# Another written order, with its PSUM slots and masks, for threshold attention followed by a three-way maxout FFN

## The chip, the cores and the metric

The kernel runs on one core of one Trainium2 chip. The metric is the device time of one execution in microseconds, as the median of several runs. The engines are PE (TensorE; its weight loads are shown as PEld), DVE (VectorE), ACT (ScalarE), POOL (GpSimd) and SP (SyncE), which issues nearly all DMAs.

## The reference

Attention over 8 batches of 8 heads, 576 rows of 64 each, in which each row of scores keeps only what lies within tau of its maximum; then an FFN whose hidden layer is the maximum of three products.

```python
scores = scale * np.matmul(q, k.transpose(0, 1, 3, 2))
thresh = np.max(scores, axis=-1, keepdims=True) - tau
scores = np.where(scores >= thresh, scores, -1000000000.0)
attn = np.exp(scores - np.max(scores, axis=-1, keepdims=True))
attn = attn / (np.sum(attn, axis=-1, keepdims=True) + 1e-09)
x = np.matmul(attn, v)                     # heads side by side: 4608 rows of 512
h = np.maximum(np.maximum(x @ w1, x @ w2), x @ w3)   # 768 wide
out = h @ w_out
```

## The kernel before

The work is cut into 16 quads (8 batches, two quads of four heads each). A quad has 9 chunks of 128 rows, each for two heads at once; a chunk has two halves r, one for each head of its pair, so there are 288 scores of 128 x 576 in all.

The functions, in the order in which a chunk meets them: `load` (SP) brings q, k and v of a quad; `transposed` (PE, tile `tp`) turns q and k, and `evacuated` (ACT for q, DVE for k) copies them to `qt` and `kt`; `swapped` (POOL, at the start DVE too) makes `qs`, q with the two halves of the partitions exchanged. `scores` (PE, tile `sc`) makes a score as two matmuls, one on each half of the array's rows, 256 columns on the one and 320 on the other, in two passes each. `maximum` (DVE) reads the score from PSUM, writes it negated to `z` and its row minimum to `nm`.

From there a score half goes one of two ways, and each way has two forms. Its digit in the string `MASKED` says which:

- 0, plain: `threshold` (DVE, a 128 x 1 instruction, `th`), `exponents` (ACT, reads `z`), `numerators` (ACT, a second pass with a sum).
- 1, masked: `exponents` (ACT, once), then `numerators` on DVE, which drops what is below exp(-tau) and sums.
- 2 and 3, direct: as 0 and 1, but ACT's `exponents` reads the score from PSUM and not from `z`; no threshold is made for 2. The bank then comes free only behind ACT.

`reciprocals` (DVE, `rs`), `normalized` (POOL, `P`) and `turned` (SP, a transposing DMA from `P` to `ptq`) follow. `product` (PE, tile `o`) multiplies with the values when all chunks of a quad have landed, and ACT or DVE copies the result to `xt`. The FFN of a batch (`ffn`) starts when both quads of it are in `xt`: 18 hidden products (`ph`, each in two steps of eight matmuls on alternating row halves), of which ACT copies one in three and DVE takes the maximum with the other two, then the output products (`po`), which ACT copies to `ob`.

All PSUM tiles share four slots of two banks each (`bank`, tags s0 to s3). What sets the order is neither a scheduler nor a planner in the kernel: the string `ORDER`, some 2,900 letters, is read from left to right, and each letter issues the next piece of its kind; `_Ordered` chains all instructions of an engine in that order. S, T, O, F and N stand for score, transposes, value product, FFN piece and ninth-chunk output, each with the digit of its slot; B is the second step of an FFN piece. m, s, e, n and k are maximum, threshold, exponents and the numerators on ACT and DVE; r, p and t reciprocals, normalized and turned; a and c copies of q and k; q the swap; h and v the copies and maxima of hidden products; x and w the copies of value products; u, j and f those of outputs; l and y loads and casts of q, k and v; g and z loads and casts of the weights, through a staging pool of two buffers; o, i and d stores. An engine works strictly in its own order, so a piece that has to wait holds all behind it on that engine.

```python
while x < len(text):
    what = text[x]
    if what in "STOFN":
        x += 1
    issue(what, int(text[x]) if what in "STOFN" else None)
    x += 1
```

Of the kernel before, what the change touches and what calls it, by code (L numbers as in the profile page):

```python
# [39 lines left out]
ORDER = """  # L40
llllllglllT0laclT1laclzllqqS0qqS1meS2mS3lmlT0enlkS1ylmlT2eamelrnpS3leqlmnyS1qcapS0emtnrcS3pmnT2qmepgrelS1qya
gS0pmelT2mqnS3tcpemqS2nlkT1eytaS0rmnT1kpermS3yS2enczrmS1qT0enmepnqtS3nprmaymgpeS0lptS2mppT0mtpS1enencnqsS3re
rmtpS0mS1penmS3lqnsS2mtperpekzllmT0tmpenkT1pgS3eearnS0petmnqrS2meqlnpS3lmnplsS2cetpremS1pS0nmplermtzeS3mnS2p
mtnpmS3rkpS1leektS0emnrpmemptS1eekS2pO3mktS0rennmpermT2pnS1wptemS3prkyO0tmeakS2pgS1enxlnrmS0lpesS2mezT3mS1np
mgntspcS2eqrseT3mtpeS0srmapS1mnT2ptS3mnqO0ceqmeO1prswnptnkS3pxS0meF1meS2zBresmT0qghF3klpF2nkBtaS1sveS0pemF3B
nyrrsmyBepT1svS0hpcT2nS3zmaS1erpgsF2mntpsBmnS3yvF1etssT0myeBprS2cnpS3mnS0ympelF2epF3lmBnzslssvS0htBrqmeS2vpn
S1gF0sepmF3teqBmF2erssvpBtnBkphF0eS1vtS3znmF2nrBmqteS1rpvBnS3pmlnF0pmgeS1qsBsrhmS3pevS2npS1mF0npsO3ermpesmO2
zewepgsskBxtT3nF1vS2nklBarS0mlphS3mtepF2sS1rmnyBmetF3pvT0eBpcnS2tzT1nvS0asmzS3temS2qeS1meF0trkpmS3lenpBmnlys
reklpF1umerpskS3upBeoketmS0uS2umpS3tesmS1qeT0myO2nqlrsnlprcO3etqsmepwS0xptS1mnF3psnmS2BlerskpS1thF0meF3pmeBF
2ktnBveBsrS1nvpS0hmyF3emF2npBrssT0eprtvBaF1kS3nqvBeF0myhyS2kyleF3mBelBvnpS2snsS0vptemS1pnF3rmpT2tnBmpeF0scS1  # L50
htBrnmpF3erT2rpvlBasS1pstvnS2pmeF0pS3emtBqnmT2S1hcqS3empF2eS0rsqmtS1epsmBeF3pmnF0stsvBeBknF2klhF1BvelS0nrvpB
emT3pS2arvS0ptnS3mpnO1smtesrkpeF2swnlrpmeT0S1qtescS3epBmnpmnT0trskS3paS1umS0ulqmeS3lmyS1nopS2smelS0rmeS3psmn
O1ypersmqO2etkpemO0lewqxlknpS3tS1keF2momS3lexF0ktT1enkBercpnsBpumN1ertkphkF3jS0rursS1empBnmF2ptS0vpS1smeF3yt
BsnsmBpnvS0pT1hmF2atT3srepS0cF1eprBsmeqF3vnByBynvplS2nsS0plmhS1mteS2mF0nF3mteS1rrspBnmS2pelvBlepF1smT0leqBvl
aS2rkhF3oqnsS0mtS1epmBeqsF2ssmtS0epvBeyF1mnF3vpBesrS0ktphBermS1npT2svO0nytmpncT3eS1wF2nrmS0aBrsmnqF3vnT1pS0c
eBptsF2mhpS1eS3pmteS0qmBeO1spmnkteF3rvnpT0BsskapS2xvS0erS1qmtnS3pmnF2mqlespmeS1rtkBepresmT3puS1cuS0ptmnS3pS2
meyS1lrekpF0tnsmempO3lekteskO2nrsmpeBkpxrnwS1uptS3muS2pnmF0yoeS1mF3lesymBtnS2srkpS1hmBeF0spveF2ertBmpT3nrsvS
1paBlmpnS0tS3qhmF1epsmS2leBymF3tevF0nBknlS1rsvpS2esmqnBF3srmhpS1epS0tmeF2pssBrempBtesvS0ynF1mT3lnpBvF0lhsrcS
2tnT1mBnF3valS2nrBsqmeF0pvS1epS2meBptsmS3eqF1hmT2peBcS3tnskT2O0arkplnmO2lerpvewptS3xkpS1nF2meF0sstreBsmpS3nv
pBnmS1tS2hmT3eF0rmpnF1cBpnBrevptT3S2apvS0qmtS3S1enmqF2esrsqmiepmleS0soykeS1plBnmemtS3ukS0uT1snrlO2cpekynO1me  # L60
ymeF3pwxskteS0keS1BrrnkopmF2pmS0BqeuurtsmF1phS3srnpS2meT0ptBmeS3ykpaN2esvempF0tS1jkpF3ermBeS2ptvnS1pmBnS0rls
hsmpS2elF3mqntS1mpF0nsrBskpeF2lsmBetBpveF1yhvS3lnkS2lesF0mytnBmBerqsS3veF2lpvnF1pBsmT0htBceF3rT2vnpBsaS0pvnF
1qmtS2nBsrnmT0pS3hrcpF2esS1mpteS0rmpS3emBpntF1svqnS0ssBmpeoT2vO3lamtneF1wS0nrlBpmeS3qsrS2hsmS0pnmF1eptS3smeB
pmF2ntS0veS3rsmnpS1BnpO0veytrempS2empS3xsmS1tekF0nsknlT2rmpBelmlpnscS3quS1umyS2eorT0kpeO3tmeyO1ewlepsmF3etka
rknS2qklT0nBmxespcS2eryF0mpF1uskpuBtnS2BhmqF3nsvS0peS2srmtpF1eBmpeF0srvnBptS2hyS3pmeF1lmeBlBevtF3nkT2S0arrvp
BnS2mphS1smpF0ntS3smnpBmeF1lsT2esvlF3nrBrcptBnvpS2eS0qmlhS1tsnprsmT3F2epmS0aptBemF3yevS1oS0nqmBnpsrS2mnF1ptv
S0epmBeS3mthS2skeF0F1snmlBeklO3ersvpnrmByepF0swT2eqtBvnqF3ssrcS1hpiBmpT0S2vaptS1snmS0pnT3mqF2tecT1BarmS3pnS1
vqeS0mF2pesrmnptmS3npT1seS0qctBeymqermpS1eS3mpuF0nmtuskS1eS2klnS3smBesrsepO1upmemO2txrkpukeO3wnkpS0xS2emF3et
rmS1pnBssspmF2hS0rtepS3mnBpmF1etS0veF3mnN2rnpBpjF0evtF2esBkBkhF1nsvS3eBmBevO3hrkS2pwnS1mnF3prmS2eptsF0mnBpsS
1sevyS2terBmpeF3svS1iyepBmoS0yhmtF2ekF3nBsmS1ersBvpnF0pmeF2BvteS1hBmF3rsS0vpeF1rknpBBmnO2vhptO0xrpnS3pwS2trm  # L70
npS0mnF3pmteF1pBeBvtS0rS2vpS3empF1ktkF0kBereskpemBkperumO2uptO3xpN1wtenkO2jrF3pxF1hpF2nvF3tvF1rhF2pvF3pvF1hF
2tvF3vF1hF2voF3vF1ohF2vF3vF1hF2vO3vO1wF2xuuF1oF0hiF3vF1vF0hF3vF1vF0hF3vF1vF0hF3vF1vF0hF3vF1vF0huF3vF1ovF3uoF
0uoN1fjdi
"""


# [753 lines left out]
```

## Time and profile before

| what | value |
|---|---|
| median of 3 runs | 446.21 us (446.2 to 446.45) |
| span of the profiled execution | 444.8 us |
| PE busy | 422.4 us (95%) |
| ACT busy | 403.0 us (91%) |
| DVE busy | 392.8 us (88%) |
| POOL busy | 311.9 us (70%) |
| DMA | 88.50 MB, mean 199 GB/s |

The profiled execution's own time is its span, 444.8 us from the first to the last instruction; the runs' median is 1.4 us longer. In the profile's lines each instruction group is written as engine, operation and out<-in by the names above; all of the kernel's own instructions carry the line L93, since `_Ordered` records them there, so one reads them by tile.

### The profile page before, as it was taken

Reading aid. Unit: us, or ns where it says so; the run is one execution under the profiler, and the core shown is the slowest. Engines: PE = TensorE matmul, PEld = TensorE weight load, DVE = VectorE, ACT = ScalarE, POOL = GpSimd, SP = SyncE. Lnnn points to the kernel's source line nnn. Section 1 sums busy time; section 2 is a strip of 40 time slices with the busy share of each in tenths; the row PEclk is TensorE's granted clock in tenths of the full one; section 3 lists DMA queues with packets and bytes.
Section 4 is the critical chain, followed back from the end, with each engine's and each line's share of the span. In section 5 each row is a group of like instructions: output and inputs, shape, how many; then the busy total and the mean of one; then the engine's idle time right before and its main releaser. Section 6 shows DMA issues by size and latency. Waiting matters only on the chain.

```text
span 444.8 us, 14254 instructions
## 1 busy us (share of the span) xinstructions
PE 422.4 (95%) x5188; PEld 320.2 (72%) x5190; DVE 392.8 (88%) x1228; ACT 403.0 (91%) x836; POOL 311.9 (70%) x420
## 2 busy tenths in 40 slices
...
GB/s 188 275 293 199 291 169 269 235 243 262 229 180 194 212 222 292 125 256 167 143 234 189 230 198 203 209 168 210 208 206 194 244 151 105 83 179 136 145 116 108
DMA packets 213959, 88.50 MB, mean 199 GB/s; under 512 B 189184, under 2 KB 202240, under 8 KB 213888
## 3 DMA queue, kind: packets, MB, share of 16 engines
...
q8 instruction: 41, 0.67, 0.6%
q10 hardware_dynamic: 528, 0.62, 0.5%
...
## 4 chain that ended last, share of the span: by engine, by line
PE 86%; ACT 5%; DVE 4%; issue 2%; DMA 1%; SPq 0%; DVEq 0%; ACTq 0%
PE ph L93 32%; PE sc L93 32%; PE po L93 10%; PE o L93 9%; ACT z L93 5%; PE tp L93 3%; DVE z L93 3%; DMA qm<-in_q_dram 1%; ACT qt L93 1%; SPq L93 0%; DVE xt L93 0%; DVE hm L93 0%; DVE stage L93 0%; DVE rs L93 0%; ACT ob L93 0%
## 5 line engine op out<-in xcount | busy, mean ns | idle before, releaser
L93 POOL TENSOR_SCALAR P<-z,rs 128x576 bf16<-128x576 f32 x250 | 200.6, 814 | 63.3 <-DVE rs L93 28.1
L93 DVE TENSOR_SCALAR_CACHE_REDUCE z<-sc 128x576 f32<-128x576 f32 x250 | 183.7, 750 | 14.8 <-PE sc L93 10.1
L93 PE MATMUL sc<-kt,qs 64*128 64x256 f32 (+2 forms) x640 | 182.6, 423 | 5.7 <-DVE z L93 2.3
L93 PE MATMUL sc<-kt,qt 64*128 64x320 f32 (+2 forms) x640 | 182.4, 433 | 5.2 <-ACT z L93 3.3
L93 PE MATMUL ph<-xt,w 64*128 64x288 bf16 (+2 forms) x2160 | 170.8, 283 | 0.1
L93 PEld LDWEIGHTS <-w 64*128 64x128 bf16 (+1 forms) x2160 | 130.1, 94 | 28.6 <-issue 4.3
L93 ACT ACTIVATE z<-z 128x576 f32<-128x576 f32 x174 | 117.6, 679 | 0.1
L93 PEld LDWEIGHTS sc<-kt,qs 64*128 64x128 f32 (+1 forms) x640 | 92.4, 180 | 25.7 <-DVE z L93 5.7
L93 ACT ACTIVATE z<-z,th 128x576 f32<-128x576 f32 x143 | 106.2, 769 | 5.0 <-DVE th L93 4.2
L93 PEld LDWEIGHTS sc<-kt,qt 64*128 64x128 f32 (+1 forms) x640 | 91.9, 179 | 19.7 <-ACT z L93 5.9
L93 DVE SCALAR_TENSOR_TENSOR z<-z 128x576 f32<-128x576 f32 x76 | 62.2, 830 | 0.5 <-ACT z L93 0.5
L93 PE MATMUL po<-wo,hT 64*128 64x512 bf16 (+3 forms) x454 | 53.5, 354 | 0.3
L93 POOL COPY qs<-qt 64x640 f32<-64x640 f32 (+3 forms) x66 | 43.0, 652 | 10.8 <-ACT qt L93 7.2
L93 ACT ACTIVATE z<-z,nm 128x576 f32<-128x576 f32 x68 | 50.6, 767 | 0.0
L93 DVE TENSOR_TENSOR hm<-ph,hm 128x576 bf16<-128x576 f32 (+2 forms) x54 | 37.0, 686 | 9.2 <-PE ph L93 8.9
L93 ACT ACTIVATE hm<-ph 128x576 bf16<-128x576 f32 (+2 forms) x54 | 31.8, 589 | 13.4 <-PE ph L93 12.8
L93 POOL TENSOR_SCALAR P<-stage,rs 128x576 bf16<-128x576 f32 x38 | 30.4, 804 | 19.3 <-ACT z L93 5.4
L93 PEld LDWEIGHTS <-hT 64*128 64x128 bf16 (+2 forms) x456 | 30.0, 95 | 16.5 <-issue 2.3
L93 DVE TENSOR_TENSOR hT<-ph,hm 128x576 bf16<-128x576 f32 (+2 forms) x54 | 37.0, 686 | 4.0 <-PE ph L93 2.3
L93 PE MATMUL o<-ptq,vb 128*64 128x64 bf16 (+2 forms) x544 | 39.0, 281 | 0.0
L93 ACT ACTIVATION_READ_ACCUMULATOR z<-z 128x1 f32 x174 | 34.3, 197 | 0.0
L93 PEld LDWEIGHTS <-vb 128*64 128x64 bf16 x544 | 23.3, 111 | 12.8 <-issue 4.9
...
## 6 DMA issues: line engine op xcount, KB each, us to landing
...
qm<-in_q_dram SPq DMA_DIRECT2D x15, 512.0 KB, 5.0
km<-in_k_dram SPq DMA_DIRECT2D x15, 512.0 KB, 5.3
out_dram<-ob SPq DMA_DIRECT2D x14, 512.0 KB, 4.0
stage<-in_moe_w_dram SPq DMA_DIRECT2D x9, 512.0 KB, 5.2
ptq<-P SPq DMA_TRANSPOSE x144, 4.0
...
stage<-in_moe_w_out_dram SPq DMA_DIRECT2D x3, 512.0 KB, 4.9
```

The costliest lines, as they stand in the source:

```text
L93: ins = fn(*a, **kw)
```

## The change

The two strings are replaced: `MASKED`, 288 digits, and `ORDER`, which has the same pieces in another order and with other slot digits. Nothing else differs; no matmul, load or store is added or taken away. The digits change in number too: 169 plain, 78 masked, 33 and 8 direct before; 184, 82, 14 and 8 now. So DVE makes 90 masked sums instead of 86, ACT 198 second passes instead of 202, and 184 thresholds stand in place of 169. Of the 41 direct reads of PSUM 37 stood ahead of the first hidden product; of 22, 13 do.

```diff
 MASKED = """
-232222322322222222021032222202332122123122200200111000000000100000000011
...
+000300021200000210020001210102023030023000211010000100000010000001001010
...
 ORDER = """
-llllllglllT0laclT1laclzllqqS0qqS1meS2mS3lmlT0enlkS1ylmlT2eamelrnpS3leqlmnyS1qcapS0emtnrcS3pmnT2qmepgrelS1qya
...
+llllllgllT2lcaqqlT2S3alcqqmgS1zsS3mesnmS1gS0emlS3snmlT2ermS0plaseslpmnlcqS1skeqlT3canmqS3zleS2mnqrmS3eplS0my
...
```

Where it moves instructions, at three places. The first is DVE's list from its third instruction of the program's start on, with the copies of the first transposes (`kt`, `qs`) and the first maxima (`z,nm<-sc`); before:

```order
L93 COPY kt<-tp 128x320
L93 COPY qs<-qt 64x320
L93 COPY qs<-qt 64x256
L93 TENSOR_SCALAR z,nm<-sc 128x576 x3
L93 TENSOR_SCALAR z,sm<-z 128x576
L93 TENSOR_SCALAR z,nm<-sc 128x576 x2
L93 RECIPROCAL rs<-sm 128x2
```

and now:

```order
L93 COPY kt<-tp 128x320
L93 COPY qs<-qt 64x320
L93 COPY qs<-qt 64x256
L93 TENSOR_SCALAR z,nm<-sc 128x576
L93 TENSOR_SCALAR th<-nm 128x1
L93 TENSOR_SCALAR z,nm<-sc 128x576
L93 TENSOR_SCALAR th<-nm 128x1
L93 TENSOR_SCALAR z,nm<-sc 128x576 x2
L93 TENSOR_SCALAR th<-nm 128x1
```

The first maxima are now followed by thresholds (`th`), which the direct form did not need; the first masked sum (`z,sm<-z`) comes later.

The second is SP's list, from the last load of the first quad's q on: `stage` are weights, `vm` and `vr` values, `q`, `qm` and `km` what `tp` needs next. Before:

```order
L93 DMA qm<-in_q_dram 64x2x512
L93 DMA vm<-in_v_dram 64x4x256
L93 DMA vm<-in_v_dram 64x4x256
L93 DMA vr<-in_v_dram 64x8x64
L93 DMA vr<-in_v_dram 64x8x64
L93 DMA q_147<-in_q_dram 128x2x64
L93 DMA k_149<-in_k_dram 128x2x64
L93 DMA qm<-in_q_dram 128x2x512
```

and now:

```order
L93 DMA qm<-in_q_dram 64x2x512
L93 DMA vm<-in_v_dram 64x4x256
L93 DMA stage<-in_moe_w_dram 128x4x256
L93 DMA stage<-in_moe_w_dram 128x4x256
L93 DMA vm<-in_v_dram 64x4x256
L93 DMA vr<-in_v_dram 64x8x64
L93 DMA vr<-in_v_dram 64x8x64
L93 DMA q_147<-in_q_dram 128x2x64
L93 DMA k_149<-in_k_dram 128x2x64
L93 DMA qm<-in_q_dram 128x2x512
```

Two weight loads have moved ahead of half of the values and of the second quad's q and k; the second of them waits for POOL, since the staging pool has two buffers.

The third is PE's list behind the first step of the first hidden product (`ph`). Before:

```order
L93 MATMUL ph<-xt,w_63 128x288
L93 MATMUL sc<-kt,qs 128x256
L93 MATMUL sc<-kt,qt 128x320
L93 LDWEIGHTS w_63
L93 MATMUL ph<-xt,w_63 128x288
```

and now:

```order
L93 MATMUL ph<-xt,w_63 128x288
L93 MATMUL tp<-identf,km 128x64 x8
L93 MATMUL sc<-kt,qt 128x256
L93 MATMUL sc<-kt,qs 128x320
L93 MATMUL sc<-kt,qt 128x320
L93 MATMUL sc<-kt,qs 128x256
L93 MATMUL tp<-identf,qm 128x64 x8
```

The transposes of keys (`tp<-identf,km`) of the fourth quad and two more scores, which stood ahead of this product, now stand behind its first step.

More of the change, by code (lines that the diff above doesn't have):

```diff
@@ L24 @@
 MASKED = """
-232222322322222222021032222202332122123122200200111000000000100000000011
-000010111020011000101000000001100001001000010011111100000000100100000000
-110010030111000100010000000001010100001110001011010100110000000000000000
-100101101011000000120000001010000000110011100000001110001000010011111021
+000300021200000210020001210102023030023000211010000100000010000001001010
+000011001100010101001000000000101000101020101111010110000000010000001001
+010011101010210100100001000100110000000001110101030110000001000000001000
+000111000111010023001000000010000000111201010011011100000011000100031312
 """
@@ L40 @@
 ORDER = """
-llllllglllT0laclT1laclzllqqS0qqS1meS2mS3lmlT0enlkS1ylmlT2eamelrnpS3leqlmnyS1qcapS0emtnrcS3pmnT2qmepgrelS1qya
[L42 to L70, printed above, removed]
@@ L71 @@
-npS0mnF3pmteF1pBeBvtS0rS2vpS3empF1ktkF0kBereskpemBkperumO2uptO3xpN1wtenkO2jrF3pxF1hpF2nvF3tvF1rhF2pvF3pvF1hF
-2tvF3vF1hF2voF3vF1ohF2vF3vF1hF2vO3vO1wF2xuuF1oF0hiF3vF1vF0hF3vF1vF0hF3vF1vF0hF3vF1vF0hF3vF1vF0huF3vF1ovF3uoF
-0uoN1fjdi
+llllllgllT2lcaqqlT2S3alcqqmgS1zsS3mesnmS1gS0emlS3snmlT2ermS0plaseslpmnlcqS1skeqlT3canmqS3zleS2mnqrmS3eplS0my
+nsmezersS1tpekS3lepT2mnlpasrmynS2ylqelT0npmlT1nspcT2arqrS3ectqeS2gmpnspS1nmT0eqmepsS1tapT3mnS2yesrS1mpeS0mtn
+pcS1ertsmpelmyepklnS1ynrsS3ptnmpeslrS2mpeT1mepS0tezmlnkqaS0ntmegrspS0npertS1mpnlknS0qsemS3qermT2tqeskS0gnpS1
@@ new lines @@
+mepcntmzO2elmnprnwS1pesmS2pterS3rmpleT0kpaS2mS1ntpssemS3lqeO0mlnkpemtxrsT3peS0cznS2rmntpeS0rpsmetpsmS2npkS3e
+tyemnS0rtmpeS2gmpnlmS0nyplskT1eS2yeO3rmtqarknpS0gsmeO1preswyemS2xtS3kpnlF0smeT1prmS2npcnS3zsmT1eBmapS2shsgF1
+qmeF3qBektBpnrS2vlnF0ympS1esBvpnS2trspmF3hlzmeBseT0svzT2tS1acgS3pnrF2mnpS0meT1qBmF3nytcpS0evBlperF1mgphS2ssk
+npS0tmeF3lBseqsmF2lnqrBveByvS1eS0ptmhS3lnpmF2nF1zsmBersS0pvnF3pmeBzBstnvS2hlrsS0pmeF3yrmpeF2tBknpS1veS0tmnBq
+gS3mnpS1lerrpsO0mepvteO3spwlnpsmleF2kyT0xS1kaBlnmS3hS0rsmpeS1tsrpS2melF3mqeT0mBynF1scnT2ptBvaS0pevS3zemS2tey
@@ new lines @@
+S1rmqnF0smtnpmeS3psBemqetkT1usS3knF2trcpusmepS1esS0ormpS3empBntmelkS1uS0lrmnpO3sukyntmO2qerwpetkS1pxlS0semS3
+lF2pnmF1lesrmBponS0rkplS3hmBleF2ymelF0sBvpeBkepF3rsntvS1BphmF2nyslpF0svnBrT3evlBaF1keS2qS3hmpBemF0qntS2rssve
+pS3mnBptrF1snvpS2emBptnS0mpF3hrmT2ptnBceF0vT1tBarsS2evlqS1nmF3pS0nsmtpBemS2qhT1ssmS0peS3cnytF2mnS1sBmetF0rve
+pF3mBeptS2srevplF1nsBmpF0ektBhkBleO2vlnrvpeT1rwpS3tnS0kpaF2snmpemtT1eS3rscpS0nmBqetmpeT1kS0arS3supmS1umtqnS0
+meqS3omS2npS1meS0rsmnpO3kemeO2ymxnpO1rwtepkeS0yS2remtpF3xsmpekS1qeS2smeBymepklnyF1T0kluBucN2hkteS0ornkpF3ljm
@@ new lines @@
+S1lBpsrsemS0lpevS2F1psmeT3tBmalF0vnT3BknS2chS1nrF0srpsmeF3prBsmeF2pnvtBqS1nsrvS0eprtmBF3qmhS1estypS2mnBpmeS0
+tpF1velS2psnmlF3pemBT0nprsvBtaS2khS1qmeS0tF3psmnF2psesmBtF1nvlS0erBsrpmnBqS3svhS0pnmF1pemT2BecyO0lpvernskpF1
+tnS3wS2eprmT0BpmaF3nsptvT0BercpS2htS1mqnS0meS3ptF2semO1lemlnskByxkF3etT0rvBaS1evpS2empS0temyS3erT1mpF2insmpn
+S0scyteBrkpelmelS3kqS1elF0mulkqulnS3smlO2epmlnkO3oerwpnkpS1xBrremqnkS3putS1smuS2epmF0eS3opmS1npsmBS2rkthpF3e
+mF0yBsrmeS1tsevpBS2nmpF3etvpT1nBmyS0ykhtS2asrmS3pnF1tsmpeF0smBeBtsrnvpF2nS3vpteS1mlF0emBeBrkpthS3ssrnS1vpF2e
@@ new lines @@
+mF0qnBmBnpssvS1thpS3emT2qF0emT1rBcpatF3nrvS1qleS2kpF0emBnpmBS1vphS2emtqF0nmT3T1eBsrcplO2avpesrktqO0ewnkS3xys
+sS1nmS2tempS0lF3erpmF1nmpBnBspvS0estF2rqsmnS3prBhmtF0pevT1lyeBpcT3nS2vaS1rstnsmS0qeS3mpF2empemqS1esktpS0nmBn
+myT3kuS0uctS1esO2rmlpelpmeO3lknrewF0ptxkpelS2rseS3oymBelmpnlkF2puS1suF3etmyBekS0S1hrmpBnmS2peN0rsmpetsvpnT2o
+kF1jS3akBtemF0nrS2vpBnmpS3hrS1sstpmeF2speF0srmBnptS3vepS1meBtqF2mnS3rveptS1snmpBkF0hiF3rnsmlpS2eBymBeptF1vnq
+lT2rssF0ecpBnvBtphS2srpnF3vF1epmBetT0vS2aBsnmlT0S3ncF2hlsmS0elrS1spmBnmS3qetS0vpeF1lmT2eBsrmapO3nskqtevF0nps
@@ new lines @@
+S2wBemS1hS3mnF2tsrnmS0pS1esmpF3eBsrmpeS0vBqnmS1tepS2mnO0rvpempS1xtsS3ynmF0nmyetkT1eS2ssrcpeS3mBperkpnS2meO1k
+yemupO3uwlnkS2oyxS1emlS0errT3mpF2nskplameT1BskqelceF0skquF1tuBrS3hpBemF2qvS0eptBmnpF3lvS1epoBrnmpS2nF0pmF1th
+skBnlT2sveS3BamS0nvS2teF3rmpS1nrmBytpF0shmS2perBsstrmpeF1kpT3nF2tvBepcBeS0tvqnS3smphS1mntT0qF2meS3parrBssmpe
+S1vnS0pS3meptF2mnF1pBsnmtyBesvS0hsS3srtmpeF2mF1pnS0keBeO3vetrmpnT2sBqcnF0rqveF2BpsnwS1hprsBmepT3S0vatS1mnqF2
+seT3mptS0ncT1qBamS3eqvS1eprS0meF2pmepmT1eBktqncnS3sktuS1rmuF0pempesS2knS1mBermtpnsS3opuS1nmO2ukemO3xokerspS0
```

5 lines of the change are left out of this document (added).

## The prediction, as it was made before the changed kernel ran

> **What bounds the kernel now.** I read the table of stretches first, with cuts at the places where PE fills up: 10.7 (ACT's first score work is under way), 73.1 (the first hidden product of the FFN), 171.1 and 273.0 (first hidden products of batches 2 and 4), 415.0 (the last batch alone). Columns: length, busy time and instructions of each engine, granted clock, DMA share, GB/s.
>
> ```profile
> 0.00:10.70 10.70, 7.91 (x70) 6.74 (x72) 3.18 (x12) 3.12 (x5) 2.18 (x9) 0.85 0.72 183
> 10.70:73.10 62.40, 48.47 (x438) 27.24 (x436) 55.11 (x168) 60.95 (x133) 54.91 (x74) 0.94 1.12 248
> 73.10:171.10 98.00, 97.94 (x1279) 76.69 (x1278) 94.89 (x305) 97.69 (x202) 81.36 (x107) 1.00 1.14 224
> 171.10:273.00 101.90, 101.81 (x1336) 80.03 (x1334) 96.58 (x310) 99.39 (x205) 75.41 (x99) 1.00 1.03 205
> 273.00:415.00 142.00, 140.89 (x1862) 111.11 (x1858) 130.76 (x411) 132.22 (x272) 95.07 (x131) 1.00 0.88 172
> 415.00:444.80 29.80, 25.38 (x228) 18.38 (x224) 12.33 (x29) 9.63 (x23) 2.93 (x4) 0.99 0.43 129
> ```
>
> There are two regimes. From 10.7 to 73.1 ACT works 60.95 of 62.40 us and PE only 48.47, at a clock of 0.94: only scores exist yet, and ACT's exponents set the pace. From 73.1 on PE works all the time. Up to 273.0 ACT (97.69 of 98.00, then 99.39 of 101.90) and DVE (94.89, then 96.58) are nearly full as well, so three engines limit at once and no stretch has room to hide much. After 415.0 PE has FFN alone.
>
> PE being busy hides a second cost. The timeline shows two scores in a row (start, length, engine, operands, idle before):
>
> ```profile
> 237.29 0.38 PE L93 MATMUL sc<-kt,qs 64*128 64x256 f32 x1
> 237.76 0.18 PEld L93 LDWEIGHTS sc<-kt,qs 64*128 64x128 f32 x1 [0.28 <-ACT hm L93]
> 237.76 0.53 PE L93 MATMUL sc<-kt,qs 64*128 64x320 f32 x1
> 238.30 0.40 PE L93 MATMUL ph<-xt,w 64*128 64x288 bf16 x3
> PEld sc L93 <- ACT z L93: 10.4, 20, 1.0
> PEld sc L93 <- DVE z L93: 8.9, 18, 1.8
> ```
>
> The first score takes 0.47 us (237.29 to 237.76), the second 0.54: its bank came free so late that its weights were not loaded ahead. PE shows no idle time, yet 0.07 us are gone. The last two lines, of the table of waits, say how often the loader idled before a score for a result of ACT or DVE: 20 and 18 times.
>
> **The change part by part.** Every matmul stays; their order, their banks and the masks change. These are the prices (lines grouped by shape: busy, mean ns):
>
> ```profile
> L93 ACT ACTIVATE z<-z,th 128x576 f32<-128x576 f32 x143 | 106.2, 769 | 5.0 <-DVE th L93 4.2 <-DVE rs L93 0.4
> L93 ACT ACTIVATE z<-z,nm 128x576 f32<-128x576 f32 x68 | 50.6, 767 | 0.0
> L93 ACT ACTIVATE z<-sc,nm 128x576 f32<-128x576 f32 x39 | 28.3, 746 | 2.9 <-DVE z L93 2.9
> L93 ACT ACTIVATE z<-z 128x576 f32<-128x576 f32 x174 | 117.6, 679 | 0.1
> L93 ACT ACTIVATION_READ_ACCUMULATOR z<-z 128x1 f32 x174 | 34.3, 197 | 0.0
> L93 DVE TENSOR_SCALAR_CACHE_REDUCE z<-sc 128x576 f32<-128x576 f32 x250 | 183.7, 750 | 14.8 <-PE sc L93 10.1 <-POOL P L93 2.6 <-issue 0.3
> L93 DVE DVE_READ_ACCUMULATOR z<-sc 128x1 f32 x250 | 20.6, 82 | 0.0
> L93 DVE SCALAR_TENSOR_TENSOR z<-z 128x576 f32<-128x576 f32 x76 | 62.2, 830 | 0.5 <-ACT z L93 0.5
> L93 DVE TENSOR_SCALAR th<-nm 128x1 f32<-128x1 f32 x169 | 22.7, 144 | 0.2
> L93 DVE COPY kt<-tp 128x640 f32<-128x640 f32 x15 | 12.2, 815 | 0.2
> ```
>
> Masks over the whole kernel: 4 more score halves take DVE's masked sum (86 to 90), 4 fewer ACT's (202 to 198), and 15 more thresholds are made (169 to 184), because direct reads fall from 41 to 22. DVE gains 4 x (0.830 + 0.08 for its accumulator) + 15 x 0.144 = 5.8 us; ACT loses 4 x (0.679 + 0.197) = 3.5 us. Where that falls decides.
>
> *Ahead of the first hidden product* (counted in the written order) stood 54 scores and 16 transposed groups, 50 first ACT passes (7 plain, 6 masked, 37 direct) and 37 second ones; now 52, 15, 49 (28, 8, 13) and 36. ACT: 21 x 0.769 + 2 x 0.767 - 24 x 0.746 - 0.876 = -1.1 us, so the product can come 1.1 us earlier. But PE has done two scores and one transposed group less, which it must do later, where it is full: 2 x 0.48 + 0.3 = 1.3 us (0.3 as in the next fence: 17.50 to 17.79 for eight transposes, and two more behind). Bounds -1.1 (PE finds room after all) and +1.3 (ACT starves somewhere and the gain is lost); I take the sum, **+0.2**.
>
> *From there to the first hidden product of batch 4* (73.1 to 273.0 now): DVE gets 4 more maxima, 2 more masked sums, 1 more copy of keys and 2 fewer thresholds: 4 x 0.832 + 2 x 0.910 + 0.815 - 0.288 = 5.7 us. ACT gets 0.6 (3 fewer plain, 4 more masked and 1 more direct pass, 1 fewer second pass), PE the 1.3 already counted. DVE's idle time there is 3.11 + 5.32 = 8.4 us; the work fits if DVE can run at 98.6%, and then this costs nothing. The most that any stretch shows is 94.89 of 98.00, 96.8%; at that share (94.89 + 96.58 + 5.7) / 0.968 = 203.7 us against 199.9 now: +3.8, of which 1.3 is PE's own. So 0 to +2.5. DVE frees most banks, and the 14.8 us that it idled before maxima were mostly waits for a score, which cannot all be filled; I take the middle, **+1.3**.
>
> *PE's transitions.* A product with the values (o) uses the array's other split, and what runs ahead of it drains:
>
> ```profile
> 17.50 0.46 PE L93 MATMUL tp<-identf,qm 64*128 64x64 f32 x8
> 17.79 0.23 PE L93 MATMUL tp<-identf,q 64*128 64x64 f32 x2
> 99.28 0.68 PE L93 MATMUL ph<-xt,w 64*128 64x288 bf16 x8
> 99.89 0.40 PE L93 MATMUL o<-ptq,vb 128*64 128x512 bf16 x1
> 73.06 0.67 PE L93 MATMUL ph<-xt,w 64*128 64x288 bf16 x8
> 73.55 0.38 PE L93 MATMUL sc<-kt,qs 64*128 64x256 f32 x1
> ```
>
> Ahead of o the eight hidden products last 0.61 us (99.28 to 99.89), ahead of a score 0.49 (73.06 to 73.55). The written order enters o 24 times instead of 22: 2 x 0.12 = **+0.2**, at least 0.
>
> *Banks.* Counting PE work at these prices between the end of one use of a bank and the start of its next, behind the first hidden product, 51 reuses had under 1.0 us of work between and 33 have now. Each of the 18 saves at most 0.07 us, -1.3 in all; at least nothing, if the release was in time or comes later because of DVE. I take half: **-0.6**. Longer queues of waits on SP, POOL's casts and the last batch (PE alone there, in the same pieces) I cost at nothing: behind 415.0 PE's work is untouched and covers ACT's 9.63 us and DVE's 12.33.
>
> *The loads.* SP now issues the second and third weight load ahead of the second half of the values and of the second quad's q and k. The third needs the staging buffer that POOL's first cast empties.
>
> ```profile
> 9.16 1.04 POOL L93 CAST w<-stage 128x1024 bf16<-128x1024 f32 x1 [7.85 <-DMA stage<-in_moe_w_dram]
> 7.72 2.00 SPq L93 DMA_DIRECT2D vr<-in_v_dram  x2
> 9.77 0.62 SPq L93 DMA_DIRECT2D q<-in_q_dram  x1
> 10.95 0.80 SPq L93 DMA_DIRECT2D qm<-in_q_dram  x1
> 11.81 0.85 SPq L93 DMA_DIRECT2D km<-in_k_dram  x1
> qm<-in_q_dram SPq DMA_DIRECT2D x2, 512.0 KB, 6.3
> km<-in_k_dram SPq DMA_DIRECT2D x1, 512.0 KB, 7.0
> ```
>
> SP stands until 10.2 (9.16 + 1.04); behind it queue half of vm, both vr (2.00), q, k, then qm and km, which so leave near 14.6 and 15.4 instead of 10.95 and 11.81, and land near 21 and 22.4 (6.3 and 7.0 later). PE wants qm at 17.50 now, with 9 scores issued; the new order puts 14 scores ahead of it, and 5 scores are worth some 7 us of ACT (0.769 + 0.679 + 0.197 for a plain one, 0.767 for a masked one), so it is wanted near 24.5. Cover: 2 to 3 us; cost 0. Without that cover it is a rival.
>
> Sum: 0.2 + 1.3 + 0.2 - 0.6 = +1.1 us on the profiled span of 444.8, so 445.9. The median of the runs, 446.21, lies 1.4 above that span; I add the same and forecast **447.3 us**.
>
> **The rivals.** What a measurement can tell from no change is 0.2%, 0.9 us.
>
> *It comes out even.* ACT's 1.1 us in the head is real, DVE's added work fits into its 8.4 us of idle time, banks and transitions cancel: 0.2 + 0 + 0.2 - 0.6 = -0.2, 446.0. For it: totals of PE are the same, ACT's fall. Against: DVE never ran above 96.8%.
>
> *Faster.* The bank order is the change's real content: waits on late banks fall by the full 1.3 us, ACT saves its 1.1 us in the head, and PE's 1.3 us are absorbed in the stretch from 273.0 (PE idles 1.1 us of 142.00 there, ACT 9.8): -1.1 - 1.3 + 0.2 + some DVE, 0.5 = -1.7, 444.5. It decides if the loader's waits for ACT and DVE fall well below 38. For it: 18 of 51 short reuses go. Against: two more scores are left for the full regime.
>
> *The loads come late (slower still).* If qm of the second quad lands 3 us later than worked out (vm's second half and the weights share the DMA engines at a share of 1.12 already), PE stands at the transposes of the second quad, and ACT, the bound there, runs dry for 1 to 4 us: 447.3 + 2.5 = 449.8. It decides from a landing behind 24.5 on.
>
> *One more spell at half clock.* The first two rows grant 0.85 and 0.94: PE lost 1.6 us of clock in 10.7 us, and 3.7 in the next 62.4. As long as ACT is the bound this is free; a spell of the size of the first row's, 1.6 us, that lies across the first hidden product would be paid: 447.3 + 1.6 = 448.9. For it: PE has even less to do in the head now. Against: the rows from 73.10 on show 1.00. The Trainium skill, TensorE: Matmul & The Clock Gate, Part 1: The HAM clock gate, says that the array's clock is halved after an idle window and that windows run free of the kernel's start; the trace agrees with a reduced clock only where PE idles, and no run here shows whether the spells move from run to run.
>
> **How the numbers follow.** Forecast (slower, about 1 us) 0.37; even 0.23; faster 0.27; late loads 0.08; half clock 0.05. Faster 0.27, within 0.2% 0.23, slower 0.50. The likeliest one's own range is 446.6 to 448.5. The range over the cases goes from 444.0, half a microsecond below the faster rival, to 450.6, 0.8 above the late loads; DVE's upper bound, 447.3 + 1.2, lies within, and some 0.15 of the chance is left outside.
>
> **What would show it.** In the changed kernel's profile: the first hidden product near 72 us if ACT's 1.1 us counts, and PE busy without a break behind it; DVE's busy sum near 398.6 and ACT's near 399.5; DVE above 97% of the stretch that follows, and the loader's waits for DVE z longer, for ACT z fewer. qm of the second quad should be issued near 14.6, and PE's wait for it be absent. The forecast is wrong if the head is longer or shorter by over 1 us, if a stretch behind 73 us shows PE idle, or if DVE takes its added work without later banks.

## The result, and the profile after

The changed kernel is slower: 450.49 us (449.5 to 453.45, four runs) against 446.33 (446.2 to 446.74) on the same chip, a ratio of 1.0097 with a 95% interval of 1.0073 to 1.0121. The forecast was 447.3 with a range up to 450.6. The direction was right, the size was not: +4.2 us instead of +1.1. The profiled execution, 453.45 us with a span of 451.6, is the longest of the four.

The table of stretches, cut at the same events as before (first score work of ACT, first hidden products of batches 0, 2 and 4, the last batch alone). Columns: length, busy time and instructions of PE, its loader, DVE, ACT and POOL, granted clock, DMA share, GB/s.

```profile
0.00:10.70 10.70, 8.81 (x80) 6.68 (x80) 4.95 (x19) 4.68 (x9) 2.86 (x9) 1.00 0.72 188
10.70:75.60 64.90, 48.93 (x410) 32.18 (x410) 53.41 (x178) 59.63 (x126) 59.43 (x77) 0.84 1.10 245
75.60:179.20 103.60, 101.69 (x1306) 76.20 (x1304) 98.44 (x313) 100.44 (x207) 79.56 (x108) 1.00 1.14 226
179.20:279.60 100.40, 99.92 (x1322) 76.66 (x1320) 97.86 (x312) 97.46 (x200) 75.57 (x100) 1.00 1.05 205
279.60:422.30 142.70, 141.00 (x1863) 106.41 (x1860) 132.24 (x413) 133.49 (x272) 94.10 (x128) 1.00 0.85 164
422.30:451.60 29.30, 25.35 (x222) 18.28 (x220) 12.19 (x26) 8.35 (x19) 1.25 (x2) 1.00 0.38 110
```

The first hidden product, forecast at 72.0, comes at 75.6 (73.1 before). From there to that of batch 4 it takes 204.1 us instead of 199.9, and from there to the end 171.9 instead of 171.8. Two parts have changed most: the head, where PE's clock fell from a mean of 0.94 to 0.84, and the next hundred microseconds, in which PE idles 1.9 us.

Which waits are new is told by the table of waits (us in total, times; PEld is PE's weight loader, and the last two rows give the longest as well):

```profile
PEld sc L93 <- DVE z L93: 15.8, 23, 1.9
PEld sc L93 <- ACT z L93: 4.1, 3, 1.8
PE sc L93 <- DVE z L93: 6.5, 10, 1.4
PE o L93 <- DMA ptq<-P: 3.9, 2, 2.5
```

The loader waits 23 times for DVE and 3 times for ACT (18 and 20 before): with fewer direct reads the banks hang on DVE. The sum of these two rows, 19.9 us, is no smaller than before (19.3). The last row had no counterpart. PE stood twice at a value product until the last transposed P of its quad had landed. PE's timeline shows the longer one (start, length, operands, idle before):

```profile
66.75 0.40 PE L93 MATMUL o<-ptq,vb 128*64 128x512 bf16 x1
69.62 2.02 PE L93 MATMUL o<-ptq,vb 128*64 128x512 bf16 x14 [2.46 <-DMA ptq<-P]
72.11 0.85 PE L93 MATMUL sc<-kt,qs 64*128 64x320 f32 x1
72.79 0.43 PE L93 MATMUL sc<-kt,qs 64*128 64x320 f32 x1
74.51 0.48 PE L93 MATMUL sc<-kt,qt 64*128 64x256 f32 x1
75.58 0.66 PE L93 MATMUL ph<-xt,w 64*128 64x288 bf16 x8
```

PE reaches the second quad's first value product at 66.75, 2.6 us earlier than the kernel before, whose row shows no idle time:

```profile
69.39 1.18 PE L93 MATMUL o<-ptq,vb 128*64 128x512 bf16 x16
```

The changed kernel gets no further until 69.62. Then the product itself runs slowly: from 69.62 to the next score are 2.5 us, and that score's matmul lasts 0.85 us where the same shape at 72.79 lasts 0.43. The other two engines pay with PE, since their copies of the product stand in their written order:

```profile
72.21 0.76 DVE L93 CAST xt<-o 128x576 bf16<-128x576 f32 x1 [2.77 <-PE o L93]
74.62 0.65 ACT L93 ACTIVATE xt<-o 128x576 bf16<-128x576 f32 x1 [4.04 <-PE o L93]
```

ACT, the bound of the head, stood for 4.04 us. Why the P landed late is in SP's list. Before, the five last transposes of that quad were issued from 56.25 on, and PE came to the product at 69.39:

```profile
55.62 0.53 SPq L93 DMA_DIRECT2D qm<-in_q_dram  x1
56.25 10.68 SPq L93 DMA_TRANSPOSE ptq<-P  x5
```

In the changed kernel two loads stand directly ahead of them, and they start at 59.34:

```profile
57.97 0.62 SPq L93 DMA_DIRECT2D vm<-in_v_dram  x1
58.64 0.60 SPq L93 DMA_DIRECT2D q<-in_q_dram  x1
59.34 7.90 SPq L93 DMA_TRANSPOSE ptq<-P  x5
```

The first of the five had its P complete at 52.5, so SP was nearly 7 us behind (5.2 in the kernel before). The last one left SP at 67.25 and landed at 69.58. In the kernel before it landed at 68.90: a margin of 0.5 us. The new order brings the product 2.6 us forward and its transposes 0.7 us back.

### The profile page after: what moved, and what is told of

It is laid out like the page before. It is cut to its first block, busy times and chain, and to the rows that moved or that the text cites. A ratio compares the mean times of both kernels' runs of the same rounds, so it can differ in the third digit from the quotient of the medians.

```text
span 451.6 us, 14298 instructions
## 1 busy us (share of the span) xinstructions
PE 425.7 (94%) x5190; PEld 316.4 (70%) x5190; DVE 399.1 (88%) x1251; ACT 404.1 (89%) x828; POOL 312.8 (69%) x420
## 4 chain that ended last, share of the span: by engine, by line
PE 79%; DVE 9%; issue 3%; DMA 3%; ACT 3%; POOL 1%; SPq 1%; DVEq 0%; POOLq 0%
PE ph L93 29%; PE sc L93 28%; PE po L93 10%; PE o L93 9%; DVE z L93 7%; PE tp L93 3%; ACT z L93 2%; DMA ptq<-P 2%; DMA qm<-in_q_dram 1%; POOL P L93 1%; SPq L93 1%; DVE stage L93 1%; DVE kt L93 1%; DVE hm L93 0%; ACT qt L93 0%
## 5 line engine op out<-in xcount | busy, mean ns | idle before, releaser
L93 POOL TENSOR_SCALAR P<-z,rs 128x576 bf16<-128x576 f32 x250 | 193.9, 786 | 79.0 <-DVE rs L93 31.0
L93 PE MATMUL ph<-xt,w 64*128 64x288 bf16 (+2 forms) x2160 | 168.9, 283 | 0.2
L93 PEld LDWEIGHTS <-w 64*128 64x128 bf16 (+1 forms) x2160 | 124.7, 94 | 32.2 <-issue 3.7
L93 ACT ACTIVATE z<-z,th 128x576 f32<-128x576 f32 x158 | 118.9, 768 | 7.6 <-DVE th L93 6.5
L93 PEld LDWEIGHTS sc<-kt,qs 64*128 64x128 f32 (+1 forms) x640 | 94.7, 181 | 23.1 <-DVE z L93 8.1
L93 PEld LDWEIGHTS sc<-kt,qt 64*128 64x128 f32 (+1 forms) x640 | 94.6, 181 | 22.1 <-DVE z L93 7.7
L93 DVE SCALAR_TENSOR_TENSOR z<-z 128x576 f32<-128x576 f32 x78 | 64.3, 830 | 0.8 <-ACT z L93 0.8
L93 POOL COPY qs<-qt 64x640 f32<-64x640 f32 (+3 forms) x66 | 49.4, 749 | 13.1 <-ACT qt L93 9.6
L93 ACT ACTIVATE z<-z,nm 128x576 f32<-128x576 f32 x70 | 52.7, 768 | 0.5 <-DVE z L93 0.5
L93 PEld LDWEIGHTS <-hT 64*128 64x128 bf16 (+2 forms) x456 | 27.0, 95 | 19.8 <-issue 2.8
```

What stands on the lines that cost most here:

```text
L93: ins = fn(*a, **kw)
```

## The experiments

Three theories stood against each other. *Transposes*: PE comes to a value product before its last transpose has landed, and the wait costs the time. *DVE*: the added maxima and masked sums make DVE the bound. *Half clock*: reduced-clock spells that move from execution to execution make the difference. All ratios are against the kernel before on the same chip; "head" is the start of the first hidden product, and the last two columns are the lengths from it to the one of batch 4 and from there to the end.

| kernel | ratio (95%) | median | span profiled | head | to batch 4 | to the end |
|---|---|---|---|---|---|---|
| before | 1 | 446.3 to 446.6 | 444.8 | 73.1 | 199.9 | 171.8 |
| changed | 1.0097 (1.0073 to 1.0121) | 450.5 | 451.6 | 75.6 | 204.1 | 171.9 |
| again | 1.0131 (1.011 to 1.0152) | 452.4 | 449.9 | 75.6 | 202.4 | 171.9 |
| o_later | 1.0131 (1.0108 to 1.0154) | 452.2 | 452.2 | 76.1 | 204.8 | 171.4 |
| t_first | 1.0123 (1.0089 to 1.0158) | 451.7 | 446.5 | 71.6 | 203.5 | 171.4 |
| t_late | 1.0081 (1.0068 to 1.0094) | 450.4 | 448.8 | 77.2 | 199.9 | 171.7 |
| t_late_fill | 1.0076 (1.0054 to 1.0098) | 449.7 | 450.4 | 78.9 | 199.8 | 171.7 |
| after_fill | 1.0093 (1.0074 to 1.0111) | 450.7 | 450.4 | 73.6 | 204.9 | 171.9 |
| before_k | 0.9972 (0.9949 to 0.9996) | 445.6 | 443.6 | 73.1 | 199.9 | 170.6 |
| t_first_k | 1.0035 (1.0021 to 1.005) | 448.4 | 447.4 | 71.4 | 205.9 | 170.1 |
| before_mask | 1.0123 (1.01 to 1.0147) | 452.0 | 450.9 | 74.4 | 203.8 | 172.7 |
| t_first_plain | 1.0114 (1.0088 to 1.0139) | 452.0 | 449.4 | 71.8 | 207.5 | 170.1 |
| before_best | 0.9978 (0.9966 to 0.9991) | 445.7 | 444.0 | 73.6 | 199.9 | 170.5 |

The span and the three lengths are of one profiled execution each, the ratio is of all executions. The old order's second stretch (to batch 4) is 199.8 to 199.9 in five profiles whose masks are untouched; the new order's is 202.4 to 204.9 in five, 205.9 and 207.5 in the other two.

### again: the changed kernel once more

> The changed kernel once more, for a second profile. Transposes theory (PE comes to the last transposed P of a quad before it has landed): a wait of an o for DMA ptq<-P of 2 to 3 us near 67 to 70 us and of 1 to 2 us near 171 us is there again, since the written order puts it there; ratio 1.008 to 1.010. Half-clock theory (the difference lies in reduced-clock spells that move from execution to execution): a mean clock of 0.984 to 0.987 as in the changed kernel's three undisturbed-looking executions (449.5 to 450.6), against 0.977 in its profiled one (453.45), goes with 2.5 to 3.5 us less. DVE theory (the added maxima and masked sums make DVE the bound): waits of PE for DVE z are as long as before, 6.5 us in all, whatever the clock.

The wait at the first place came back, 2.02 us at 67.07; the second, near 171 us, did not (the transpose landed at 169.5 for a product at 170.2). The head was again 75.6. PE's waits for DVE z were 6.4 us. The clock theory fell as far as the mean clock goes: executions at 0.992 took 451.27 and 452.44. The ratio, forecast at 1.008 to 1.010, was above the one of the first session, though the profiled span is 1.7 us shorter, by about the second wait.

What the clock does do is seen in stretches of 3.41 us cut where the recorded clock changes. The changed kernel, the two around the wait:

```profile
65.95:69.36 3.41, 1.20 (x15) 0.64 (x11) 3.41 (x13) 3.41 (x9) 3.21 (x5) 1.00 1.07 179
69.36:72.78 3.42, 3.16 (x22) 1.96 (x22) 0.65 (x2) 1.22 (x2) 3.42 (x5) 0.50 0.99 313
```

And the same kernel in this run:

```profile
66.30:69.71 3.41, 1.40 (x18) 0.78 (x16) 3.41 (x13) 3.41 (x9) 3.21 (x5) 1.00 0.95 170
69.71:73.12 3.41, 3.41 (x22) 1.78 (x18) 0.81 (x2) 1.19 (x2) 3.41 (x5) 0.50 1.08 337
```

Both times PE works 1.2 to 1.4 us of one stretch, and the next one is granted at 0.50. The kernel before, which does not wait there, keeps its clock:

```profile
65.53:68.94 3.41, 2.81 (x30) 2.03 (x32) 3.32 (x13) 3.38 (x7) 3.25 (x6) 1.00 1.10 165
68.94:72.36 3.42, 3.42 (x47) 1.81 (x47) 3.42 (x11) 3.42 (x10) 3.20 (x5) 1.00 0.96 320
```

This spell does not move freely: it follows the wait.

### o_later: the value products behind more scores

```diff
-...S2yeO3rmtqarknpS0gsmeO1preswyemS2xtS3k...
+...S2yermtqarknpS0gsmepresyemS2O3O1wxtS3k...
-...O3kemeO2ymxnpO1rwtepkeS0yS2...
+...O3kemeymxnprtepkeS0O2O1wyS2...
```

> The changed kernel with its value products of the second quad of batch 0 put behind the next two scores, and those of the sixth quad of the program behind the next score; nothing else moves. Transposes theory: PE does these 2 and 1 scores while the transposes land, the waits for DMA ptq<-P (2.46 and 1.45 us) fall to at most 1.5 and 1.0, and the time falls by 1.0 to 2.5 us against the changed kernel: ratio 1.004 to 1.007. DVE theory: the scores in front need banks that DVE frees late, so the wait only changes its name; ratio 1.009 to 1.011.

No product waited any more, and nothing was won: the head came at 76.1, ratio 1.0131. The two scores now in front wait for banks that DVE frees (0.97 and 0.72 us; at the second place the one score in front waits 1.34), PE works 1.72 us of a stretch, and the next is at half clock all the same:

```profile
67.27:70.68 3.41, 1.72 (x18) 0.78 (x16) 3.41 (x14) 3.41 (x8) 3.21 (x5) 1.00 0.96 267
70.68:74.10 3.42, 3.42 (x22) 1.44 (x24) 0.73 (x3) 1.15 (x2) 3.42 (x5) 0.50 1.11 280
```

That is what the DVE theory had said of this place: DVE was busy all 3.41 us. PE has no other work there that is ready, so moving the product only renames the wait. A cure has to be sought where the wait starts, at the transposes.

### t_first: the transposes ahead of the loads

SP's loads of values are put behind the transposes at both places; POOL's casts of the first of them follow later too.

```diff
+    def late_values():
+        each = [load(g, first=g == 0) for g in range(NQ)]
+        for g in range(NQ):
+            if g == 4:
+                for _ in range(4):
+                    yield next(each[4])
+                yield from each[3]
+            if g == 3:
+                yield next(each[3])
+                yield next(each[3])
+            else:
+                yield from each[g]
-                 l=(None for g in range(NQ) for _ in load(g, first=g == 0)))
+                 l=late_values())
 ORDER = """
-...S3rmpleT0k...ssemS3lqeO0m...preswyemS2xtS3kpnlF0...vlnF0ympS1...F3nytc...
+...S3rmpeT0k...ssemS3qeO0m...preswemS2xtS3kpnlllF0...vlnF0mpS1...F3nyyytc...
-...hkBleO2vlnrvpe...S1umtqnS0...
+...hkBeO2vnrvpe...S1umtllqnS0...
```

> The changed kernel with SP's loads of values that stood ahead of the last five transposes of the second and of the sixth quad put behind them (two loads each; POOL's casts of the first of them follow later too); PE, ACT and DVE keep their order. Transposes theory, with SP's queue as its cause: the last transpose lands 1.3 to 2.6 us earlier, the waits of o for DMA ptq<-P (2.46 and 1.45 us) shrink to under 1.0 each, and the time falls by 1.5 to 3.5 us against the changed kernel: ratio 1.002 to 1.006. If DMA bandwidth and not the issue queue limits, the landing moves by less than 0.7 us and the ratio stays at 1.008 to 1.010. DVE theory: no change, 1.009 to 1.010.

The profile did what the transposes theory says. The last transpose landed at 66.3 instead of 69.4, PE's list of waits holds no o that waits for a transpose, no stretch behind 50 us is at half clock, and the head came at 71.6, 4.0 us earlier, with a span of 446.5:

```profile
65.57:68.98 3.41, 3.38 (x40) 2.09 (x40) 3.41 (x13) 3.41 (x10) 3.21 (x6) 1.00 0.95 232
68.98:72.40 3.42, 3.42 (x47) 2.35 (x44) 3.42 (x11) 3.14 (x6) 3.42 (x5) 1.00 1.09 288
```

The ratio did not follow: 1.0123 against a forecast of 1.002 to 1.006, no better than the 1.0131 of again. The profiled execution, 448.25, is the fastest of six that reach 454.31. A margin of 0.8 us at the product (66.3 to 67.1) is less than the 1.9 us by which one landing moved between two profiles (t_late and t_late_fill), so the other executions may have waited; their profiles were not taken.

### t_late: the same wait put into the kernel before

```diff
-...kyO0tmeakS2pgS1enxlnrmS0lpesS2...
+...kyO0meakS2pgS1enxlnrmS0ltpesS2...
```

> The kernel before, with one thing moved: the last transpose of the second quad is issued behind three more loads on SP. Transposes theory: it lands 1.5 to 2.5 us later (68.9 in the kernel before, first value product at 69.4), PE waits 1 to 2 us for DMA ptq<-P there, and the kernel is slower by 1 to 3 us: ratio 1.002 to 1.007. If such a wait ahead of the first hidden product is made up for later (ACT runs on, PE catches up), the ratio is 1.000 to 1.001. DVE and half-clock theories: no change, 1.000.

One transpose moved behind three loads: it lands at 71.9, PE waits 2.06 us, and the kernel is 3.6 us slower by its ratio, more than the wait and above the forecast of 1 to 3 us, which had no price for the clock. The head moves from 73.1 to 77.2, and all that follows takes as long as before (199.9 and 171.7). The half-clock stretch is there again:

```profile
69.46:72.88 3.42, 1.36 (x17) 0.81 (x18) 1.87 (x7) 3.10 (x8) 3.20 (x6) 1.00 1.15 303
72.88:76.30 3.42, 3.42 (x29) 2.00 (x26) 1.79 (x3) 0.17 (x1) 1.96 (x3) 0.50 1.24 140
```

So one late transpose at this place costs 4.1 us in the profile, in a kernel with none of the change's masks or banks.

### t_late_fill and after_fill: the wait filled with work

Matmuls that nobody reads stand ahead of the waiting product (32 in slot 0 and 36 in slot 3, `W` in the order ahead of the product's letter).

```diff
+        elif what == "W":
+            warm = bank("warm", 3)
+            some = vrs[0].rearrange("p h d -> p (h d)")[:, 0:128]
+            for _ in range(36):
+                tensor.matmul(warm[:, 0:128], some, some, start=True, stop=True)
```

> The kernel with the late transpose (ratio 1.0081, a wait of 2.06 us for DMA ptq<-P at 69.5 and a half-clock spell of 3.41 us that begins at 72.9), with 32 matmuls of 128 columns on values at hand put ahead of the waiting value product, some 1.8 us of PE work that nobody reads; leaves nothing out. If the spell comes from the idle time within the clock's own window: no spell behind 50 us, the loss ahead of the first hidden product falls by about 1.7 us (half of 3.41), ratio 1.0035 to 1.0055. If the spells come at their own times: the spell stays, ratio 1.007 to 1.009. If the wait alone had cost nothing and the spell all: ratio 1.000 to 1.001.

> The changed kernel with 36 such matmuls (some 2.0 us) ahead of the value product that waits 2.0 to 2.5 us. Idle theory of the spell: the spell at 69.4 to 73.1 is gone, the product and the score behind it last 1.3 and 0.5 us instead of 2.6 and 1.0, the first hidden product starts near 73.9 instead of 75.6; ratio 1.0060 to 1.0095 against 1.0131 of the changed kernel on the same day. Own-time theory: spell and ratio stay, 1.011 to 1.015.

after_fill separates the two parts of the cost. The transpose landed at 69.1 (69.4 in again), and the product ran from 68.7 on; but the clock held, and the head came at 73.6 instead of 75.6:

```profile
65.73:69.14 3.41, 3.30 (x51) 2.59 (x48) 3.40 (x13) 3.41 (x8) 3.21 (x5) 1.00 1.04 170
69.14:72.55 3.41, 3.41 (x45) 1.94 (x44) 1.93 (x4) 1.12 (x2) 3.41 (x5) 1.00 1.01 321
```

The three executions did not start alike, so I count from PE's arrival at the product (in after_fill, at the filling in front of it): 67.07 to 75.59 in again, 8.5 us; 66.44 to 73.59 in after_fill, 7.15; 67.10 to 71.62 in t_first, where nothing waits, 4.5. Of the 4.0 us some 2.5 are the wait and some 1.5 the clock that follows it; the landing, 0.2 us later in after_fill by this count, leaves that much open. The runs show this less surely: its ratio, 1.0093, lies below the 1.0131 of again, but cannot be told from the 1.0097 of the same program's first session. t_late_fill missed its forecast: in its profiled execution the transpose landed at 73.8, 1.9 us later than in t_late, so 2.39 us of waiting were left behind the filling, and a half-clock stretch from 73.31 to 76.72 came after it. That execution, 452.19, is the slowest of its six (448.52 the fastest). Its ratio, 1.0076, cannot be told from t_late's. It shows how far a landing can move (71.9 to 73.8 with the same list on SP), and that a fixed filling does not cover that.

### before_k: a masked sum that POOL holds up

Looking for a loss that the kernel before has alone I found DVE at 277 us. A masked sum (`numerators` on DVE, two operands in SBUF) lasts 2.60 us, and the score that waits for the maximum behind it comes late; the last two rows are POOL's at that time:

```profile
277.13 2.60 DVE L93 SCALAR_TENSOR_TENSOR z<-z 128x576 f32<-128x576 f32 x1
279.73 0.74 DVE L93 TENSOR_TENSOR hm<-ph,hm 128x576 bf16<-128x576 f32 x1
```

```profile
280.52 0.48 PE L93 MATMUL sc<-kt,qs 64*128 64x256 f32 x1 [0.94 <-DVE hm L93]
```

```profile
276.94 1.46 POOL L93 TENSOR_SCALAR P<-z,rs 128x576 bf16<-128x576 f32 x2
278.38 0.74 POOL L93 TENSOR_SCALAR P<-stage,rs 128x576 bf16<-128x576 f32 x1
```

```diff
-...S3ykpaN2esvempF0...
+...S3ypaN2esvemkpF0...
```

> The kernel before with one masked sum on DVE (half 96, 1; it lasted 2.60 us at 277.13 instead of 0.75 while POOL ran P back to back) put behind the hidden maximum and the score maximum that stood behind it. If DVE's masked sum is held up by POOL's running instructions and the two maxima (which read PSUM) are not: the maxima come 1.8 us earlier, the score that waited 0.94 us for DVE hm at 280.5 no longer waits, and the kernel is 0.8 to 1.8 us faster: ratio 0.996 to 0.998. If the 1.85 us belong to that place whatever runs there (an instruction fetch), the next instruction is late instead, and the ratio is 0.999 to 1.001.

The hidden maximum now runs at 277.24 while POOL works as before, and the masked sum lasts 1.15 us:

```profile
277.24 0.76 DVE L93 TENSOR_TENSOR hm<-ph,hm 128x576 bf16<-128x576 f32 x1
278.59 1.15 DVE L93 SCALAR_TENSOR_TENSOR z<-z 128x576 f32<-128x576 f32 x1
```

The length from batch 4 on falls from 171.8 to 170.6, all else is equal to a tenth, and the ratio is 0.9972: faster than both kernels. So the time does not belong to the place but to that kind of instruction beside POOL, as far as this one place shows.

### t_first_k: transposes still earlier, and that masked sum moved

As t_first, with the load of the ninth rows of q behind the transposes as well, and the changed kernel's longest masked sum (2.21 us at 342.7) behind two hidden maxima.

```diff
-...O0mlnkpemt...S0rtmpeS2g...F1kpT3n...S0tvqnS3s...
+...O0mnkpemt...S0rtlmpeS2g...F1pT3n...S0tvkqnS3s...
```

> The changed kernel with transposes ahead of the values' loads at both places as in t_first, one more load (the ninth rows of q) behind the five transposes, and the masked sum that held DVE for 2.21 us at 342.7 put behind two hidden maxima. Transposes theory, with landing times that vary by 1 to 2 us from execution to execution as the reason why t_first scattered from 448.25 to 454.31: the last transpose lands 1 us earlier still (65.3 instead of 66.3, product at 67.1), nearly all executions are like the fast one of t_first, and the loss of 1.27 us at 343.9 falls below 0.4: ratio 1.001 to 1.004. If the scatter has another cause: some executions stay above 452, ratio 1.008 to 1.014.

It landed at 65.2, the head came at 71.4, and from batch 4 on it takes 170.1 instead of 171.9. All nine executions lie between 446.9 and 449.4, none near the 454 of t_first; ratio 1.0035, as forecast. This agrees with the scatter theory: 1.7 us of margin at the product where t_first had 0.8. The two edits were not run apart, so it is not shown that the margin alone took the scatter away; some 1.8 us of the gain stand behind batch 4, where the masked sum was moved. Its second stretch, 205.9, was longer in this profile (1.2 us of waiting for a bank of DVE at 143, among others), for a reason that no run isolates.

### before_mask and t_first_plain: DVE's load alone

```diff
 MASKED = """
-...0...
+...1...
 ORDER = """
-...F2mntpsBmnS3yvF1e...2cnpS3mnS0ympe...
+...F2mntpBmnS3yvF1e...2cnpS3mkS0ympe...
```

Six halves like this one, spread from the first hidden product of batch 0 to that of batch 4; t_first_plain has the reverse in t_first_k (1 to 0, k to n, an s added).

> The kernel before with six plain halves between the first hidden products of batches 0 and 4 made masked (their second pass runs on DVE in place of ACT, their thresholds fall away); nothing else moves. DVE gets 6 x (0.83 + 0.08 - 0.144) = 4.6 us more there, ACT 6 x 0.876 = 5.3 us less, about what the change does to DVE in this stretch (5.7). DVE theory of the prediction (DVE nearly full, so its added work comes through in part): the loss between the two products, 7.8 us in the kernel before, grows by 0.5 to 2.0 us; ratio 1.001 to 1.0045. If DVE has room, or ACT is the tighter one: 0.999 to 1.0005, and the loss stays within 0.3 of 7.8.

> The changed kernel with its transposes first and the one masked sum moved (t_first_k, ratio 1.0035), and six masked halves between the first hidden products of batches 0 and 4 made plain: DVE gets 4.6 us less there, ACT 5.3 us more. DVE theory: the loss of that stretch (12.5 us in t_first_k's profile, 9.1 to 11.6 in the other profiles of the new order) falls by 0.5 to 2.0 us, ratio 1.000 to 1.0025. If ACT is the tighter one: 1.0035 to 1.007. If neither: 1.003 to 1.0045.

before_mask, from the one product to the other, and the same stretch of the kernel before:

```profile
74.36:278.16 203.80, 201.00 (x2610) 156.22 (x2609) 196.21 (x620) 194.22 (x394) 158.92 (x206) 1.00 1.08 205
```

```profile
73.06:272.99 199.93, 199.78 (x2610) 156.76 (x2609) 191.50 (x614) 197.12 (x406) 156.80 (x206) 1.00 1.08 214
```

DVE works 4.7 us more, ACT 2.9 less, and the stretch is 3.9 us longer, where I had expected 0.5 to 2.0 us: in this order DVE's added work comes through at 0.8 of its price. (The 1.3 us more in the head and the 0.9 more behind batch 4 stand where the two programs are alike; the ratio, 1.0123 against a forecast of 1.001 to 1.0045, holds them too.) The reverse does not win it back: t_first_plain's stretch is 1.6 us longer than t_first_k's, its ratio 1.0114 against a forecast of at most 1.007. I read this as both engines being without room: in these two orders, work moved to either side costs time.

### before_best: more margin for the kernel before

before_k with one load more moved: q of batch 2 behind the second quad's last transpose.

```diff
-...S3rkpS1leektS0...prkyO0tmeak...
+...S3rkpS1eektS0...prkyO0tlmeak...
```

> The kernel before with the one masked sum moved (before_k, ratio 0.9972) and with the load of q for batch 2 (0.5 MB) put behind the last transpose of the second quad instead of ahead of its last five. Transposes theory: the last transpose, which landed at 68.9 for a product at 69.4, lands 0.6 to 1.5 us earlier; in the profiled execution that changes nothing, but executions in which it lands late (447.9 to 452.2 in three of some thirty of the kernel before) become rarer: ratio 0.996 to 0.9975, none above 447. If the scatter has another source: the same ratio, and single executions above 447 as before. If q now comes late for its transposes near 75.5: a wait of PE for DMA qm, ratio 0.998 to 1.002.

Ratio 0.9978, like before_k, with twelve executions from 444.4 to 447.1, like before_k's twelve (444.9 to 447.1). The second edit brought the last transpose to 66.6 (68.9 before) and shows no effect of its own on the time; whether late landings make the longest executions of the kernel before is neither shown nor refuted.

## Where the prediction was wrong, and where it was right

*The step that failed* reads: "Longer queues of waits on SP, POOL's casts and the last batch ... I cost at nothing." The head's SP queue cost 4.0 us in the profile, the wait and the clock behind it together: without it the head comes at 71.6 (t_first) instead of 75.6 (again), and t_late, which puts the same wait into the old order, shows 4.1. I had looked at the loads that SP issues near 10 us, where it was the loads that would be late, and not at the transposes that queue behind loads at 59 us. The rows for it were in the profile before: the five transposes issued from 56.25 to 66.93 for a product at 69.39. A margin of 0.5 us is a bound, and the written order alone shows that the product had moved towards it: between the letter of the quad's last transpose and that of its first product stood 9 scores, now 3.

*The half-clock rival* was put at 0.05, as a matter of chance ("whether the spells move from run to run"), and at 1.6 us. It is some 1.5 us of the 4.0, and no chance: in after, again and t_late it follows a wait of 2.0 to 2.5 us. It should not have been a rival of its own but a part of the price of such a wait. The sum of this step is some 2.5 + 1.5 instead of 0.

*The head without it.* ACT's -1.1 us: forecast 72.0, measured 71.6 and 71.4 in t_first and t_first_k. That agrees, though it proves little: the old order's own head, in programs that are alike up to there (before, before_k, before_mask), came between 73.1 and 74.4. ACT's busy sum did not fall to 399.5, though; it rose from 403.0 to 404.06. The durations added up did fall, by 4.8 us, but neighbouring instructions overlap (in the kernel before two first passes of 0.77 us start at 275.92 and 276.59, 0.67 apart), and the means that I multiplied count that overlap twice.

*The stretches behind the head.* Forecast 1.3 (PE's work left over) + 1.3 (DVE) + 0.2 (transitions) - 0.6 (banks), or 371.7 + 2.2 = 373.9 from the first hidden product to the end. Again shows 202.4 + 171.9 = 374.3, but it is the lowest of the new order's five profiles with these masks and masked sums in place: the other four show 374.9 to 376.8. So this part of the sum, +2.2, was too small as well (+2.5 to +5.0), and that again fits within 0.4 us is luck. Its members were not measured one by one; the banks' -0.6 shows in no sum of waits. DVE's busy sum came out at 399.09 (398.6 forecast). That DVE takes its work nearly for free (1.3 us for 5.7) can at best be true of the new order: before_mask pays 3.9 us for 4.7. The new order's own stretch also varies from 202.4 to 204.9, where the old one stays within 0.15 us, and that the prediction did not see. The waits of PE name much of it: in again no wait over 0.42 us stands in this stretch; in the changed kernel's first profile 1.45 at the product near 172 us, and the 1.7 us between the two profiles of this one program arise there; in o_later 1.34 at the same place; in after_fill 0.48 and 0.97 at two other products (103 and 125 us) and 0.70 for a bank of DVE; in t_first_k 1.21 for such a bank. After_fill's rows, then t_first_k's:

```profile
PE o L93 <- DMA ptq<-P: 1.5, 2, 1.0
PE ph L93 <- DVE z L93: 0.7, 1, 0.7
PE ph L93 <- DVE z L93: 1.2, 1, 1.2
```

So the products behind the head are short of margin too. Why a wait comes in one execution and not in the next stays open.

*The loads late* did not come about. SP's list at the start, and PE's transposes of the second quad:

```profile
10.07 0.37 SPq L93 DMA_DIRECT2D stage<-in_moe_w_dram  x1
14.43 0.68 SPq L93 DMA_DIRECT2D qm<-in_q_dram  x1
```

```profile
20.80 0.46 PE L93 MATMUL tp<-identf,qm 64*128 64x64 f32 x8
```

qm is issued at 14.43 (14.6 forecast) and landed at 20.3 (21). It was wanted at 20.8, not at 24.5: the cover was 0.5 us and not 2 to 3.

Put together: 445.9 was forecast for the span; with 4.0 for SP's queue it is 449.9, the span of again. In the medians SP's queue explains less: t_first_k, without that wait, has 1.0035, and about 1.0075 if the 1.8 us of the moved masked sum are added back (an estimate from these two numbers), or 3.4 us where 1.1 were forecast. In its profile the rest lies between the first hidden product and that of batch 4 (205.9 us instead of 199.9). Two of the prediction's own signs of being wrong were there: the head longer by 2.5 us, and PE idle for 1.9 us in the stretch behind it. That the measured 450.49 lies inside the range is luck: its upper end, 450.6, was set for loads that come late, and they did not.
